# Where to sum the nine exponentials of batch 5: nine small TensorE products, or two VectorE reductions inside the gates of batch 4

## The chip, the cores and the metric

The kernel runs on one core of one Trainium2 chip. The metric is the time of one execution on the device in microseconds (us). Three runs of the kernel before took 235.49, 235.75 and 235.82 us; their median, 235.75 us, is the time that the change is held against.

A core has four computing engines that run side by side, each through its own instructions in their order. TensorE (PE) multiplies matrices; its weight loads are counted apart (PEld). VectorE (DVE) and ScalarE (ACT) work along rows of data, and both can read the accumulators (PSUM). GpSimd (POOL) does such work too. SyncE (SP) starts transfers (DMA). PSUM is used here as eight banks of 128 x 512 float32.

## The reference, cut to what matters

```python
def _attn_ref(q, k, v, phi):              # 8 batches, 8 heads, 576 positions, 64 wide; 32 memory slots
    a = phi - np.max(phi, axis=2, keepdims=True)
    a = np.exp(a)
    a = a / (np.sum(a, axis=2, keepdims=True) + 1e-09)      # sum over the 576 positions
    k_m = np.einsum('bhsm,bhsd->bhmd', a, k)
    v_m = np.einsum('bhsm,bhsd->bhmd', a, v)
    scores = np.matmul(q, k_m.transpose(0, 1, 3, 2)) / np.sqrt(64)
    ...                                   # softmax over the 32 slots
    return np.matmul(attn, v_m)

def _moe_ref(x, w_gate, w_val, w_out):    # 4608 tokens, 512 -> 1536 -> 512
    g = x @ w_gate
    silu = g * (1.0 / (1.0 + np.exp(-g)))
    return (silu * (x @ w_val)) @ w_out
```

The change concerns one sum: `np.sum(a, axis=2)`, for batch 5 alone. The kernel first adds up exp(phi)k and exp(phi)v, and divides by that sum afterwards.

## The kernel before, where the change touches it

The kernel goes through the batches one after the other. While the gates and values of batch b are computed, the memory sums of batch b+1 are slipped in between. In SBUF a head's 576 positions lie as 64 rows of 9 positions, two heads above each other in 128 rows, so that the exponentials of a batch are one tile `ephi` of 128 rows x 9 x (4 x 32). The sum over 576 positions is then a sum over the nine, followed by a sum over 64 rows, which a product with a matrix of ones does.

Banks of PSUM are taken from a queue and put back at its end, **in the order of the program text**. A product that takes a bank waits on the chip until its last user has read it.

```python
    free = [f"B{n}" for n in range(8)]
    def bank(shape, dtype, name):
        tag = free.pop(0)
        ...
    def done(*tiles):
        for t in tiles:
            free.append(held.pop(id(t))[0])
```

Where GpSimd adds the nine up, it leaves a pair: the sum rounded to bf16, and what the rounding lost. Where it doesn't (batches 2, 3 and 5), nine products do the whole sum.

```python
    def phi_sum(b):                                          # on GpSimd
        e = ephis[b].rearrange("p j i m -> p j (i m)")
        wait_for(atts[b - 1, 1][0:1, 0, 0:1])
        t = att.tile([128, 4, 128], FP32, tag="es", bufs=1, name="t_es")
        ...                                                  # 8 terms, then 4, 2, 1, then the ninth
        hl = att.tile([128, 2, 128], BF16, tag="ehl", bufs=1, name="t_ehl")
        nc.gpsimd.tensor_copy(out=hl[:, 0], in_=t[:, 0])
        nc.gpsimd.tensor_tensor(out=hl[:, 1], in0=t[:, 0], in1=hl[:, 0], op=ALU.subtract)
        esums[b] = hl

    def kv_denominators(b, p):                               # line 258
        ...
        if b in esums:
            hl = esums.pop(b)
            terms = [hl[:, t] for t in range(2)]             # two products
        else:
            terms = [ephis[b][:, j].rearrange("p i m -> p (i m)") for j in range(JK)]   # nine
        for n, x in enumerate(terms):
            nc.tensor.matmul(p, lhsT=x, rhs=ones2, start=(n == 0), stop=(n == len(terms) - 1))

    def kv_items(b, beside=None):
        def run_sums():
            o = 2 * D
            p = [bank([128, CH], FP32, f"p_kv{g}") for g in range(NG)]
            behind = b in esums
            if not behind:
                kv_denominators(b, p[0][:, o:o + NG])
            kv_sum(b, p, (0, 1))                             # line 230: 72 products
            if behind:
                beside()
                kv_denominators(b, p[0][:, o:o + NG])
            kv_reciprocal(b, p[0][:, o:o + NG])              # line 262, VectorE
            kv_norm(b, p)                                    # line 266: four VectorE copies, then done(p[g])
            if beside and not behind:
                beside()
        return [run_sums, lambda: kv_T(b)]
```

`beside()` is a round of products of the feed-forward weights with the memory values (line 465, four banks, emptied in the order ScalarE, ScalarE, VectorE, ScalarE: lines 485 and 489), and two units of output products (line 719). So `behind` settles more than a count: with it the banks `p_u` are emptied before the banks `p_kv`, without it after.

A slot of the gates: two products for the gate and a Silu on ScalarE (line 525), and for the slot before it two products for the value and a multiplication on VectorE (line 531). Each takes a bank and gives it back.

```python
    def gv_slot(b, s):
        n = len(pend)
        gv_gate(b, s)          # bank, 2 products, Silu, done(gate); the value's part is put in pend
        flush_mul(n)           # bank, 2 products, VectorE multiplication, done(val)
```

In the gates of batch 4 the output products of four batches' leftover rows (`quad`) run as well. Their first sum, `p_oa`, is taken from its bank by VectorE on line 788 (`leftover("c11")`), and GpSimd makes the twelve terms they need in `quad_sums(0)`, 128 x 256 each, as soon as `t_A` of batch 4 is there. The program of a batch is woven from streams by `spread`: every stream's items are set at even distances between two marks of the 24 slots.

```python
        g = gv_slots(b)
        ...
        streams = [(g, 0, 24), (quad[:12], 0, 3), (quad[12:], 12, 18.5)]
        streams += [(outs, 4, 7 if quad else 24)]
        ...
        if not last:
            if b > 2:
                load_qT(b + 1)
            if b > 2 and b != 4:
                phi_sum(b + 1)
            streams += [
                (kv_items(b + 1, lambda: (u_item(b, 2, "aava")(), run(take(2)))), KV, KV + 4),
                ...
            ]
        spread(*streams)
```

Of the kernel before, what the change touches and what calls it, by code (L numbers as in the profile page):

```python
# [9 lines left out]
FP32 = mybir.dt.float32  # L10
BF16 = mybir.dt.bfloat16
# [3 lines left out]
def kernel(  # L15
# [19 lines left out]
    nc = tc.nc  # L35
    AF = mybir.ActivationFunctionType
    ALU = mybir.AluOpType
# [18 lines left out]
    att = ctx.enter_context(tc.tile_pool(name="att", bufs=2))  # L56
# [57 lines left out]
    def load_qT(b):  # L114

        qTs[b] = att.tile([128, NS, 128], BF16, tag="qT", name="t_qT")
        nc.sync.dma_start_transpose(out=qTs[b], in_=qs[b])
# [50 lines left out]
    ephis, rSs, bkvs, kTs, es, atts = {}, {}, {}, {}, {}, {}  # L168

    def phi_exp(b):  # L170
        t = att.tile([128, JK, NP, M], BF16, tag="ephi", name="t_ephi")
        nc.scalar.activation(
            out=t.rearrange("p j i m -> p i j m"),
            in_=phis.pop(b).rearrange("p i (j m) -> p i j m", m=M),
            func=AF.Exp,
        )
        ephis[b] = t
# [25 lines left out]
    esums = {}  # L203

    def phi_sum(b):
# [6 lines that stand above are left out]
        add = lambda o, x, y: nc.gpsimd.tensor_tensor(out=o, in0=x, in1=y, op=ALU.add)  # L212
        add(t, e[:, 0:4], e[:, 4:8])
        add(t[:, 0:2], t[:, 0:2], t[:, 2:4])
        add(t[:, 0], t[:, 0], t[:, 1])
        add(t[:, 0], t[:, 0], e[:, 8])
        hl = att.tile([128, 2, 128], BF16, tag="ehl", bufs=1, name="t_ehl")
        nc.gpsimd.tensor_copy(out=hl[:, 0], in_=t[:, 0])
        nc.gpsimd.tensor_tensor(out=hl[:, 1], in0=t[:, 0], in1=hl[:, 0], op=ALU.subtract)
        esums[b] = hl  # L220

    def kv_sum(b, p, parts):


        w0, w1 = parts[0], parts[-1] + 1
        n = (w1 - w0) * D
        for j in range(JK):
            for i in range(NP):
                for g in range(NG):
                    nc.tensor.matmul(  # L230
                        p[g][32 * i:32 * i + 32, 0:n],
                        lhsT=phi_of(b, g, j, i),
                        rhs=kvs[b][64 * g:64 * g + 64, w0:w1, i, j * D:(j + 1) * D],
                        start=(j == 0),
                        stop=(j == JK - 1),
                        tile_position=(64 * g, 32 * i),
                    )
# [54 lines left out]
# [9 lines that stand above are left out]
            kv_sum(b, p, (0, 1))  # L301
# [3 lines that stand above are left out]
            kv_reciprocal(b, p[0][:, o:o + NG])  # L305
            kv_norm(b, p)
# [4 lines that stand above are left out]
# [241 lines left out]
    def subtract(eng, out, x, y):  # L552
        eng.tensor_tensor(out=out, in0=x, in1=y, op=ALU.subtract)  # L553

    def weight_sums(c, part=(0, 1, 2, 3)):

        if 0 not in part:
            t = Ts[c]
            for n in part:
                x, y = Ts[c, n]  # L560
                subtract(nc.vector, t[:, n], x, y)
            return
        home = dict(tag=f"mphi{c}", bufs=1) if c < 2 else dict(tag="T2", bufs=1)
        t = att.tile([128, 4, 2, DM // 2], BF16, name="t_T", **home)
        w = WOc[c].rearrange("p (m e) f -> p e m f", e=2)
        h = DM // 2
        B11, B12, B21, B22 = (w[:, e, :, h * n:h * n + h] for e in range(2) for n in range(2))
        Ts[c] = t
        for n, xy in enumerate(((B12, B11), (B22, t[:, 0]), (B22, B12), (B21, t[:, 1]))):
            Ts[c, n] = xy  # L570
            if n in part:
                subtract(nc.vector, t[:, n], *xy)
# [62 lines left out]
    def wait_for(x):  # L635

        t = att.tile([1, 1], BF16, tag="mark", bufs=1, name="t_mark")
        nc.gpsimd.tensor_copy(out=t, in_=x)
# [182 lines left out]
    def q_items(b, evac):  # L821
        return [lambda n=n: q_T(b, n, evac[n]) for n in range(3)]
# [13 lines left out]
    def u_values(b):  # L836

        u_round(b, (((1,), 1, (0, 1)),), "aa")
    def run(items):
        for x in items:  # L840
            x()
# [10 lines left out]
    def exp_tables():  # L852
        nc.scalar.preload_act_table_set("natural_log_exp_and_others")
# [111 lines left out]
    def take(n):  # L965
        nonlocal backlog
        n = max(0, min(n, len(backlog)))
        part, backlog = backlog[:n], backlog[n:]
        return part
# [3 lines left out]
    def loads(b):  # L973

        if b < B:
            load_q(b)
            load_phi(b, nc.gpsimd)
            load_k(b)
            load_v(b)
# [7 lines left out]
    for b in range(2, B):  # L987
        last = b + 1 == B
        exp_tables()
        if b == 2:  # L990
            load_qT(3)
            phi_exp(2)
            (zero, ops0), (one, ops1) = products(0, ("c11",)), products(1, ("p1", "c11"))
            kv, q2 = kv_items(2), q_items(2, "aaa")
            run(zero[:6])
            sums = {n: f for n, f in zip(((1, 1), (0, 2), (1, 2)), late)}
            late.clear()
            sums[0, 2]()
            weight_sums(0)
            weight_sums(1)  # L1000
            run(zero[6:12] + one[:6] + kv[:1] + q2[:2])
            weight_sums(2, (0, 1))
            run(zero[12:16] + zero[18:22] + kv[1:] + q2[2:] + zero[16:18] + zero[22:24])
            weight_sums(2, (2, 3))
            ops0["c11"]()
            ops1["p1"]()
            wait_for(Ts[2][0:1, 3, 0, 0:1])
            for part in ((0, 1), (3,), (2,)):
                for c in (1, 2):
                    sums[1, c](part)  # L1010
            loads(4)
            backlog = one[6:12] + zero[36:] + one[12:36]
            ops = ops1
        else:
            run(take(6))
        for g in range(NG):
            scores(b, g)
        if b > 2:
            ops["p1"]()
            u_values(b)  # L1020
        else:
            run(zero[24:36] + take(6))
        run(take(6))
        z_inv_v(b, 0)
        ops["c11"]()
        run(take(6))
        if not last:
            phi_exp(b + 1)
        z_inv_v(b, 1)
        if b > 2:  # L1030
            norm(b, 0)
            norm(b, 1)
        run(take(6))
        run_late()
        if b == 4:
            wait_for(atts[4, 1][0:1, 0, 0:1])
            quad_sums(0)
        nc.scalar.preload_act_table_set("silu_and_others")
        run(take(6))
        if b == 2:  # L1040
            norm(2, 0)
        run(take(6))
        if b == 2:
            norm(2, 1)
            u_three(2)
            run(one[36:])
        g = gv_slots(b)
        quad = []
        if b == 4:
            quad = products(b, (), 0)[0]  # L1050
        if last:
            rest, rest_ops = products(b, (), 1)
            backlog += rest[:12]
        beside = 0 if last else 2 if quad else min(4, len(backlog))
        outs = [lambda: run(take(1)) for _ in range(len(backlog) - beside)]
        streams = [(g, 0, 24), (quad[:12], 0, 3), (quad[12:], 12, 18.5)]
        streams += [(outs, 4, 7 if quad else 24)]
        if b == 2:
            streams += [([lambda: u_values(2)], 2.5, 3)]
        if last:  # L1060
            streams += [([u_item(b, 2)], 5, 6)]
        if not last:
            if b > 2:
                load_qT(b + 1)
            if b > 2 and b != 4:
                phi_sum(b + 1)
            streams += [
                (kv_items(b + 1, lambda: (u_item(b, 2, "aava")(), run(take(2)))), KV, KV + 4),
                ([lambda: (u_three(b + 1), run(take(2)))], 19, 20),
            ]  # L1070
        spread(*streams)
        flush_mul()
        units, ops = products(b, ("p1", "c11"))
        backlog += units
# [34 lines left out]
```

The softmax here doesn't subtract the row's maximum and nothing guards it: scores larger than these inputs give would overflow.

## Time and profile before

| what | before |
|---|---|
| time, median of 3 (lowest, highest) | 235.75 us (235.49, 235.82) |
| span of the profiled run | 233.8 us |
| TensorE busy (weight loads) | 224.5 us, 96% (169.9 us, 73%) |
| VectorE, ScalarE, GpSimd busy | 183.2 us (78%), 173.5 us (74%), 140.6 us (60%) |
| clock granted to TensorE | full in all 40 slices |
| line 258 with exponentials, 128 x 2 | 27 products, 163 ns each |
| line 258 with the pair, 128 x 2 | 6 products, 165 ns each |
| GpSimd term for `quad`, 128 x 256 bf16 | 658 ns each |

The profile page gives the busy time of each engine, the chain of work that ended last, and the costliest groups of instructions by source line. The timeline lists instructions in order of time: start in us from the span's start, length, engine, line, operation, what is written and read, the shape, and in brackets the idle time before it with what ended it. Equal neighbours are merged into one line with a count. Ends of products overlap the starts of the next ones, so lengths of TensorE are not added up: **differences of starts** tell its pace.

### The profile page before, as it was taken

What the parts mean: (1) busy time and instruction counts of PE and PEld (TensorE: products, weight loads), DVE (VectorE), ACT (ScalarE), POOL (GpSimd) and SP (SyncE); (2) the same over time, 40 slices, a digit from 0 to 9 for tenths busy, and PEclk for the clock granted to TensorE, in tenths of its full rate; (3) what the DMA queues carried; (4) which work ended last, traced back from release to release, by engine and by line L of the source; (5) the groups of instructions that cost most, each with busy time, mean ns of one, the idle gap of its engine ahead of it and who ended that gap; (6) DMA issues with size and microseconds to landing.
All of it is one profiled execution on the core that took longest, in us unless ns stands there. A gap on an engine that the chain in (4) does not pass through costs nothing.

```text
span 233.8 us, 7201 instructions
## 1 busy us (share of the span) xinstructions
PE 224.5 (96%) x2825; PEld 169.9 (73%) x2825; DVE 183.2 (78%) x421; ACT 173.5 (74%) x369; POOL 140.6 (60%) x190
## 2 busy tenths in 40 slices
PE   7997899999999999999999999999999999999992
PEld 2554466778887776878788787877788778878881
DVE  4056799999966698989797767999799879977732
ACT  2759798988547889968896658968897789677220
POOL 8422536998199059665966688464745494039390
PEclk9999999999999999999999999999999999999999
DMA  6999999999995993999199946995024502201224
GB/s 213 210 210 206 200 206 207 231 236 266 205 241 134 261 251 47 231 227 151 35 259 212 190 128 121 254 217 94 15 78 110 106 0 94 90 35 57 62 76 136
DMA packets 36610, 36.84 MB, mean 158 GB/s; under 512 B 14560, under 2 KB 30944, under 8 KB 36576
## 3 DMA queue, kind: packets, MB, share of 16 engines
q0 software_dynamic: 16272, 22.42, 51.5%
q1 hardware_dynamic: 19536, 13.18, 23.6%
q10 hardware_dynamic: 768, 0.79, 1.1%
q8 instruction: 22, 0.36, 0.6%
q14 instruction: 12, 0.10, 0.1%
HBM read 42.47 MB, written 9.44 MB: 222 GB/s over the span
## 4 chain that ended last, share of the span: by engine, by line
PE 88%; DMA 7%; POOL 1%; ACT 1%; DVE 1%; issue 1%; POOLq 0%
PE p_v L508 21%; PE p_g L508 21%; PE p_os L719 20%; PE p_oc L719 10%; DMA t_kv<-in_v_dram 7%; PE p_u L465 5%; PE p_oa L719 5%; PE p_kv L230 2%; PE p_g L389 1%; POOL t_kv L99 1%; PE p_mT L318 1%; PE p_warm L866 1%; PE p_q L376 0%; POOL t_q L108 0%; DVE t_kT L332 0%
## 5 line engine op out<-in xcount | busy, mean ns | idle before, releaser
L531 DVE TENSOR_TENSOR t_h<-t_sg,p_v 128x288 bf16<-128x288 bf16 x192 | 81.9, 452 | 17.3 <-PE p_v L508 7.4
L508 PEld LDWEIGHTS <-t_U 128*128 128x128 bf16 x768 | 73.6, 98 | 23.2 <-issue 3.8
L525 ACT ACTIVATE t_sg<-p_g 128x288 bf16<-128x288 f32 x192 | 74.0, 424 | 17.8 <-PE p_g L508 11.5
L508 PE MATMUL p_g<-t_A,t_U 128*128 128x288 bf16 x384 | 77.1, 286 | 0.5 <-ACT t_U L487 0.5
L508 PE MATMUL p_v<-t_A,t_U 128*128 128x288 bf16 x384 | 77.2, 286 | 0.0
L719 PEld LDWEIGHTS <-t_S 128*128 128x128 bf16 x384 | 37.5, 98 | 4.5 <-issue 0.2
L596 POOL TENSOR_TENSOR t_S<-t_h 128x512 bf16<-128x512 bf16 x17 | 19.6, 1155 | 32.5 <-DVE t_h L531 30.4
L719 PEld LDWEIGHTS <-t_h 128*128 128x128 bf16 x288 | 27.1, 98 | 8.6 <-issue 5.0
L485 ACT CAST t_U<-p_u 128x512 bf16<-128x512 f32 x53 | 28.0, 607 | 6.6 <-PE p_u L465 6.6
L719 PE MATMUL p_os<-t_T,t_S 128*128 128x256 bf16 x192 | 23.7, 273 | 0.0
L553 POOL TENSOR_TENSOR t_S<-t_S,t_h 128x512 bf16<-128x512 bf16 x17 | 19.6, 1154 | 1.3
L553 POOL TENSOR_TENSOR t_S<-t_h,t_S 128x512 bf16<-128x512 bf16 x16 | 18.4, 1151 | 0.0
L553 POOL TENSOR_TENSOR t_S<-t_h 128x512 bf16<-128x512 bf16 x16 | 18.4, 1150 | 0.0
L465 PE MATMUL p_u<-W,t_kT 64*32 64x512 bf16 (+1 forms) x416 | 15.8, 364 | 0.6 <-DVE t_kT L332 0.6
L866 PE MATMUL p_warm<-bones 128*128 128x512 bf16 x44 | 13.8, 457 | 1.7 <-DVE bones L888 1.7
L719 PE MATMUL p_os<-t_T,t_h 128*128 128x256 bf16 x96 | 14.8, 273 | 0.0
L489 DVE CAST t_U<-p_u 128x512 bf16<-128x512 f32 x19 | 12.4, 684 | 1.9 <-PE p_u L465 1.9
L445 DVE TENSOR_TENSOR t_A<-t_E,t_lz 128x576 bf16<-128x576 bf16 x16 | 11.4, 739 | 0.7 <-ACT t_lz L421 0.7
L719 PE MATMUL p_oc<-t_T,t_S 128*128 128x256 bf16 x96 | 12.0, 273 | 0.0
L719 PE MATMUL p_oa<-WO,t_h 128*128 128x256 bf16 x96 | 11.8, 273 | 0.0
L719 PE MATMUL p_oc<-WO,t_S 128*128 128x256 bf16 x96 | 11.8, 273 | 0.0
L719 PE MATMUL p_os<-WO,t_h 128*128 128x256 bf16 x96 | 11.8, 273 | 0.0
(106 smaller groups left out, 308.8 us busy)
## 6 DMA issues: line engine op xcount, KB each, us to landing
out_dram<-t_o SPq DMA_DIRECT2D x15, 512.0 KB, 3.8
t_kv<-in_k_dram POOLq DMA_DIRECT2D x8, 576.0 KB, 10.2
t_q<-in_q_dram POOLq DMA_DIRECT2D x8, 576.0 KB, 8.6
t_kv<-in_v_dram POOLq DMA_DIRECT2D x8, 576.0 KB, 14.9
t_phi<-in_phi_dram POOLq DMA_DIRECT2D x6, 576.0 KB, 8.3
WO<-in_moe_w_out_dram POOLq DMA_DIRECT2D x3, 512.0 KB, 19.3
W<-in_moe_w_gate_dram POOLq DMA_DIRECT2D x2, 512.0 KB, 16.4
W<-in_moe_w_val_dram POOLq DMA_DIRECT2D x2, 512.0 KB, 16.2
```

What stands on the lines that cost most here:

```text
L230: nc.tensor.matmul(p[g][32 * i:32 * i + 32, 0:n], lhsT=phi_of(b, g, j, i), rhs=kvs[b][64 * g:64 * g + 64, w0:w1, i, j * D:(j + 1) * D], st ...
L445: nc.vector.tensor_tensor(out=a, in0=es.pop((b, g)), in1=lzs.pop((b, g)), op=ALU.mult)
L465: nc.tensor.matmul(p[g][32 * i:32 * i + 32, o:o + n], lhsT=kTs[b][64 * g:64 * g + 64, 2, 32 * i:32 * i + 32], rhs=w_part(w, c, i, g, halve ...
L485: nc.scalar.copy(out=t, in_=p)
L489: nc.vector.tensor_copy(out=t, in_=p)
L508: nc.tensor.matmul(p[:, 0:HALF], lhsT=Us[b, c, g][:, o // 2, which, 128 * (o % 2):128 * (o % 2 + 1)], rhs=atts[b, g][:, r], start=(g == 0) ...
L525: nc.scalar.activation(out=sg, in_=gate[:, 0:HALF], func=AF.Silu)
L531: nc.vector.tensor_tensor(out=dst, in0=sg, in1=val[:, 0:HALF], op=ALU.mult)
L553: eng.tensor_tensor(out=out, in0=x, in1=y, op=ALU.subtract)
L596: eng.tensor_tensor(out=t[:, 0], in0=A21, in1=A22, op=ALU.add)
L719: nc.tensor.matmul(mine[home][:, u], lhsT=lhs(c, m, u), rhs=rhs(c, m), start=fresh and u == 0, stop=(k == 5), skip_group_check=u == 1 or n ...
L866: nc.tensor.matmul(p[:, 0:128 * a], lhsT=bones, rhs=x.to_broadcast([128, a, 128]) if a > 1 else bones, start=True, stop=True,)
```

## The change

GpSimd is taken up by `quad_sums` in the gates of batch 4, so batch 5 was left without the pair. The change has VectorE make it there instead: two reductions over nine elements, each of 64 of the 128 columns, a copy that rounds to bf16, and a subtraction. They are a stream of three items over the first three slots of the gates of batch 4. Since `esums` then holds batch 5, `kv_items` takes its `behind` branch for it as it does for batches 4, 6 and 7.

```diff
+    def phi_sum_items(b):
+        e = ephis[b].rearrange("p j i m -> p (i m) j")
+        t = att.tile([128, 4, 128], FP32, tag="es", bufs=1, name="t_es")
+        hl = att.tile([128, 2, 128], BF16, tag="ehl", bufs=1, name="t_ehl")
+        esums[b] = hl
+        def half(n):
+            cols = slice(64 * n, 64 * n + 64)
+            nc.vector.tensor_reduce(
+                out=t[:, 0, cols], in_=e[:, cols], axis=mybir.AxisListType.X, op=ALU.add
+            )
+        def split():
+            nc.vector.tensor_copy(out=hl[:, 0], in_=t[:, 0])
+            subtract(nc.vector, hl[:, 1], t[:, 0], hl[:, 0])
+        return [lambda: half(0), lambda: half(1), split]
...
-            if b > 2 and b != 4:
+            if b == 4:
+                streams += [(phi_sum_items(b + 1), 0, 3)]
+            elif b > 2:
                 phi_sum(b + 1)
```

As built, VectorE's program in these slots becomes: reduction, multiplication 0, reduction, multiplication 1, copy, subtraction, the sum of line 788, multiplications 2 to 5. Before it was: multiplications 0 and 1, line 788, multiplications 2 to 5. TensorE loses nine products ahead of the 72 of line 230 and gets two behind the products of `beside`. GpSimd's program is the same, and so is the order of the transfers.

## The prediction

> **What bounds the kernel now.** I read the chain of work that ended last first. Nearly all of it is TensorE, from about 21 us on almost without a break, so a microsecond that TensorE saves or loses near 130 us should reach the end.
>
> ```profile
> ## 4 chain that ended last, share of the span: by engine, by line
> PE 88%; DMA 7%; POOL 1%; ACT 1%; DVE 1%; issue 1%; POOLq 0%
> ```
>
> Then the timeline of TensorE about the memory sums of batch 5, which now begin with the nine products:
>
> ```profile
> 129.72 0.38 PE L719 MATMUL p_os<-t_T,t_h 128*128 128x256 bf16 x2
> 129.94 0.37 PE L258 MATMUL p_kv<-ones,t_ephi 128*128 128x2 bf16 x9
> 130.23 0.80 PE L230 MATMUL p_kv<-t_kv,t_ephi 64*32 64x128 bf16 x72
> 131.41 0.61 PE L719 MATMUL p_os<-t_T,t_h 128*128 128x256 bf16 x4
> 131.88 0.42 PE L508 MATMUL p_g<-t_A,t_U 128*128 128x288 bf16 x2
> 132.33 0.42 PE L508 MATMUL p_v<-t_A,t_U 128*128 128x288 bf16 x2
> ```
>
> The nine hold TensorE for 130.23 - 129.94 = 0.29 us. A pair of 288-wide products takes 0.245 us from start to start (111.81 and 112.05 in the same timeline), but the last two lines are 0.45 apart: 0.205 us is a stall. The waits list puts it down to VectorE's copies of `p_kv`, and the timeline of VectorE shows them filling 131.29 to 132.28. The bank of that value product is the second `p_kv` bank.
>
> The same passage for batch 4, whose pair GpSimd made, is the picture that the change aims at:
>
> ```profile
> 103.46 0.41 PE L508 MATMUL p_v<-t_A,t_U 128*128 128x288 bf16 x2
> 103.80 0.80 PE L230 MATMUL p_kv<-t_kv,t_ephi 64*32 64x128 bf16 x72
> 105.43 0.19 PE L258 MATMUL p_kv<-ones,t_ehl 128*128 128x2 bf16 x2
> 105.48 0.41 PE L508 MATMUL p_g<-t_A,t_U 128*128 128x288 bf16 x2
> 105.72 0.41 PE L508 MATMUL p_v<-t_A,t_U 128*128 128x288 bf16 x2
> ```
>
> Here the two cost 0.05 us and gate and value are 0.24 apart: no stall. But 0.095 us passes idle before the 72 (they could start at 103.46 + 0.245 = 103.705), which the nine now cover.
>
> Last, what VectorE and GpSimd do where the new work goes. In the first lines VectorE waits for the value products; the sum of line 788 follows on multiplication 1; GpSimd works without a pause, one term each (128.47 - 126.59) / 3 = 0.627 us:
>
> ```profile
> 126.23 0.45 DVE L531 TENSOR_TENSOR t_h<-t_sg,p_v 128x288 bf16<-128x288 bf16 x1 [0.59 <-PE p_v L508]
> 127.15 0.45 DVE L531 TENSOR_TENSOR t_h<-t_sg,p_v 128x288 bf16<-128x288 bf16 x1 [0.47 <-PE p_v L508]
> 127.53 0.42 DVE L788 TENSOR_TENSOR t_o<-p_oa,t_p 128x256 f32<-128x256 f32 x1
> 126.59 1.91 POOL L553 TENSOR_TENSOR t_Q<-t_Q,t_x 128x256 bf16<-128x256 bf16 x3
> 128.47 1.92 POOL L553 TENSOR_TENSOR t_x<-t_x 128x256 bf16<-128x256 bf16 x3
> ```
>
> **What the Trainium skill says.** "SBUF — State Buffer", section Who interferes with whom: VectorE and GpSimd share a pair of ports as an exclusive lock; a VectorE instruction with two SBUF inputs contends with a GpSimd instruction that reads SBUF, a copy may, and tensor_reduce never does. The trace has such a meeting: GpSimd's copies of `t_x` beside VectorE's sums `t_S`, both inputs of which lie in SBUF. The sum before the copies takes 0.42 us, those beside them 0.62 and 0.64, each ending about 0.3 us behind a copy's end, and the copies slow down too: the two engines take turns.
>
> ```profile
> 55.48 0.42 DVE L596 TENSOR_TENSOR t_S<-t_h 128x512 bf16<-128x512 bf16 x1
> 55.93 0.62 DVE L553 TENSOR_TENSOR t_S<-t_S,t_h 128x512 bf16<-128x512 bf16 x1
> 56.48 0.64 DVE L553 TENSOR_TENSOR t_S<-t_h 128x512 bf16<-128x512 bf16 x1
> 55.82 1.57 POOL L585 COPY t_x<-t_h 128x256 bf16<-128x256 bf16 x3
> ```
>
> "VectorE: DVE Perf Modes", sections on the errata and the tier table: tensor_reduce runs at one element a cycle, and an instruction at that rate lasts (N + 151) / 0.96 ns. For N = 576 that gives an estimate of 757 ns. The trace has no plain tensor_reduce, but three other forms over 576 elements agree: 764 ns for the transposing reduction, 778 for the transposition, 739 for the product `t_A`. The next instruction starts before the recorded end, some 0.07 to 0.08 us earlier (the transposition at 122.35 lasts 0.78, its follower starts at 123.06).
>
> **The change, part by part.** *On TensorE.* From the first free moment to the second of the two gate and value products: now 132.33 - 129.94 = 2.39 us; in the pattern of batch 4, 105.72 - 103.705 = 2.015 us. The saving is 0.375 us: nine products less two, 0.24; the stall, 0.205; against that the 0.095 of idle time that comes into the open; the rest, 0.025, is rounding and small gaps. All of it is on the path.
>
> *On VectorE,* estimates from the durations above. The last sum of the output products starts at 124.96 and lets a follower start at 125.56. Reduction 125.56 to 126.24 (757 ns less 0.08); multiplication 0 at 126.24, against 126.23 before; reduction from 126.61; multiplication 1 at 127.29, against 127.15; copy at 127.66. Up to here the idle gaps of 0.59 and 0.47 us take the work nearly whole. Now the split. If the ports were free: copy of 128 elements to 127.95 at most ((128 + 151) / 0.96 = 0.29 us), subtraction to about 128.25, line 788 from 128.17 to 128.59. With the ports taken: GpSimd's terms run from 127.22 to 127.87 and from 127.84 to 128.50. The copy comes out at about 127.97 either way (held until 127.87, then short; or not held, 0.29 us). The subtraction, asked for at 128.0, finds GpSimd in its next term and waits for its end at 128.50 to 128.58; it ends near 128.7, and line 788 runs from 128.65 to 129.07.
>
> *What line 788 sets free.* I follow the queue of banks. When the first `quad` sum has its bank, the queue is 3, 4, 7, 2, 0, 6. Gate 0 takes 3, gate 1 takes 4, value 0 takes 7, `p_oa` takes 2, gate 2 takes 0, value 1 takes 6; the banks come back in the order 3, 4, 7, 0, 6, 2. So gate 3 and value 2 take 3 and 4, gate 4 and value 3 take 7 and 0, gate 5 takes 6, and **value 4 takes bank 2**, which line 788 frees. Value 4 starts at 128.76 now. From the end of a bank's reader to the product is about 0.055 us (the last `p_kv` copy ends at 132.28, the product starts at 132.33). So line 788 may end by 128.70. Free ports: 128.59, no stall. Taken ports: 129.07 + 0.055 = 129.12, a stall of 0.36 us, or 0.29 if the copy leaves GpSimd's term alone. The banks of multiplications 2 and 3 come free by about 129.5 and 129.9 and are asked for again near 129.8 and 130.4: in time.
>
> *The sum.* Free ports: -0.375 us. Taken ports: -0.375 + 0.29 to 0.36, that is -0.02 to -0.09. In both cases a change within two tenths of a percent.
>
> **The rivals.**
> 1. *The whole gain arrives* (-0.4 us): 235.4. For it: tensor_reduce stays off the shared ports, and 0.11 us is in hand when nothing contends. The lock may also be held for less than a GpSimd term's recorded 0.66 us, so that the subtraction slips in.
> 2. *The stall moves* from the `p_kv` bank to bank 2, and the gain is nearly used up: 235.65 to 235.75. For it: GpSimd is busy without a gap in just this window, and the meeting at 56 us shows the turn-taking. Against it: that was a copy, this is a GpSimd sum.
> 3. *The reductions are slower than one element a cycle,* since each reads nine elements 128 apart and writes 64 results. At 0.9 us each from start to start, multiplication 1 slips to 127.74, the copy meets the next term, the subtraction the one after it, and line 788 ends near 129.75: a stall of about 1.0, the time near 236.4. Against it: the other reading forms over 576 elements keep to the estimate.
> 4. *TensorE's gain is hidden anyway,* behind a transfer or GpSimd. Against it: the transposing transfer of batch 5's keys is issued at 135.26, behind stores that SyncE issues first, three us after its data were ready, and its first reader comes at 141.84; GpSimd has nearly 2 us idle after its terms (1.96 before 134.22).
>
> **Range and chances.** I give the first rival 35%, the second 45%, the third 15%, the fourth 5%. Weighted with -0.37, -0.06, +0.5 and 0 that is -0.08, so I predict 235.65 us. The three runs before are spread over 0.33 us, so the medians add some 0.15 us. The range is 235.2 to 236.1. Nothing here moves the time by 2%, which would be 4.7 us: faster 0.005, within 2% 0.985, slower 0.01.
>
> **What the changed profile would show.** Right: no stall between the first gate and value after the two products, their starts 0.24 to 0.26 us apart; about 1.78 us from TensorE's first free moment to that gate, against 1.94 before; reductions of 0.74 to 0.78 us; multiplication 0 still at 126.2. The second rival shows as a subtraction of more than 0.5 us and a gap before value 4 on TensorE, ended by line 788; the first as a subtraction of about 0.3 us and no such gap; the third as reductions of 0.9 us or more. The prediction is wrong if value 4 waits for over 0.8 us, if the multiplications of VectorE still lag when `p_u` is emptied, or if the saving near 132 us is gone again by the scores of batch 5 near 145 us.

## The result, and the profile after

The changed kernel takes **241.77 us** (median of six runs, 241.22 to 242.39), the kernel before 235.78 us beside it. The ratio is 1.0255, with a 95% interval of 1.0236 to 1.0273. The prediction was 235.65 us, in a range up to 236.1.

The chain of work that ended last, of the changed kernel: TensorE's share falls from 88% to 78%, and VectorE's rises from 1% to 6%.

```profile
PE 78%; DMA 8%; DVE 6%; POOL 2%; issue 2%; ACT 2%; DVEq 0%; POOLq 0%; ACTq 0%
```

The timeline of VectorE in the gates of batch 4 shows the new instructions (line numbers from 222 on are 19 higher than before):

```profile
125.49 1.15 DVE L231 TENSOR_REDUCE t_es<-t_ephi 128x64 f32<-128x576 bf16 x1
...
126.92 1.14 DVE L231 TENSOR_REDUCE t_es<-t_ephi 128x64 f32<-128x576 bf16 x1
127.97 0.45 DVE L550 TENSOR_TENSOR t_h<-t_sg,p_v 128x288 bf16<-128x288 bf16 x1
128.34 3.94 DVE L236 CAST t_ehl<-t_es 128x128 bf16<-128x128 f32 x1
132.31 0.29 DVE L572 TENSOR_TENSOR t_ehl<-t_es,t_ehl 128x128 bf16<-128x128 f32 x1
132.52 0.42 DVE L807 TENSOR_TENSOR t_o<-p_oa,t_p 128x256 f32<-128x256 f32 x1
```

The copy of 128 columns is recorded with 3.94 us. The timeline of GpSimd in the same passage:

```profile
128.41 1.91 POOL L572 TENSOR_TENSOR t_x<-t_x 128x256 bf16<-128x256 bf16 x3
130.28 1.91 POOL L572 TENSOR_TENSOR t_Q<-t_x,t_Q 128x256 bf16<-128x256 bf16 x3
```

Its last term ends at 130.28 + 1.91 = 132.19; the copy ends at 128.34 + 3.94 = 132.28, 0.09 us later. Line 807 is line 788 of before: it frees bank 2 five us later than it did. On TensorE's timeline value 4 stands behind it. First gate 5 and value 4 before, then the same passage after:

```profile
128.52 0.41 PE L508 MATMUL p_g<-t_A,t_U 128*128 128x288 bf16 x2
128.76 0.41 PE L508 MATMUL p_v<-t_A,t_U 128*128 128x288 bf16 x2
```

```profile
128.48 0.40 PE L527 MATMUL p_g<-t_A,t_U 128*128 128x288 bf16 x2
132.99 0.64 PE L527 MATMUL p_v<-t_A,t_U 128*128 128x288 bf16 x2 [4.11 <-DVE t_o L807]
...
133.85 0.68 PE L527 MATMUL p_g<-t_A,t_U 128*128 128x288 bf16 x2
134.33 0.68 PE L527 MATMUL p_v<-t_A,t_U 128*128 128x288 bf16 x2
```

In the changed kernel they are 4.51 us apart where 0.245 is usual: 4.27 us of waiting. Behind it a gate and its value are 0.48 apart and last 0.68, not 0.41. The table by stage says why: its columns are the busy time of each engine (with the number of instructions), and behind them the granted clock of TensorE, the DMA share and GB/s.

```profile
128.00:132.70 4.70, 0.88 (x8) 0.58 (x6) 4.67 (x5) 0.82 (x2) 4.19 (x7) 1.00 1.18 182
132.80:136.10 3.30, 3.11 (x70) 2.02 (x74) 1.77 (x5) 0.41 (x1) 0.00 (x0) 0.50 0.63 139
136.20:139.00 2.80, 2.63 (x60) 1.69 (x41) 2.01 (x7) 2.26 (x6) 0.00 (x0) 1.00 0.01 1
```

TensorE works at half clock from 132.81 to 136.22 us, for 3.41 us. I compared the starts of the gates and values in the two traces. From 26 us up to this passage the changed kernel leads by a constant 0.06 us. Value 4 then starts 4.23 us late, the lag reaches 5.76 us at the gate at 138.84, and it is 5.76 up to the last product. So the passage costs 5.76 + 0.06 = 5.82 us, and nothing after it gives or takes. Each trace here has such a constant lead or lag from 26 us up to the passage, at most 0.3 us, which arises ahead of 26 us; where a passage is weighed below, it is taken off.

### The profile page after: what moved, and what is told of

Same layout as the page of the kernel before. It is cut to its first block, busy times and chain, and to the rows that moved or that the text cites. A ratio compares the mean times of both kernels' runs of the same rounds, so it can differ in the third digit from the quotient of the medians.

```text
span 239.6 us, 7193 instructions
## 1 busy us (share of the span) xinstructions
PE 225.6 (94%) x2818; PEld 170.3 (71%) x2818; DVE 189.4 (79%) x425; ACT 173.8 (73%) x369; POOL 140.6 (59%) x190
## 4 chain that ended last, share of the span: by engine, by line
PE 78%; DMA 8%; DVE 6%; POOL 2%; issue 2%; ACT 2%; DVEq 0%; POOLq 0%; ACTq 0%
PE p_v L527 20%; PE p_g L527 19%; PE p_os L738 18%; PE p_oc L738 9%; DMA W<-in_moe_w_gate_dram 8%; PE p_u L484 5%; PE p_oa L738 4%; PE p_kv L249 2%; DVE t_ehl L236 2%; DVE t_h L550 1%; DVE t_o L768 1%; POOL t_kv L99 1%; POOL t_kv L103 1%; DVE t_z L447 1%; PE p_g L408 1%
## 5 line engine op out<-in xcount | busy, mean ns | idle before, releaser
L738 PE MATMUL p_os<-t_T,t_h 128*128 128x256 bf16 x96 | 15.3, 279 | 0.0
L885 PE MATMUL p_warm<-bones 128*128 128x512 bf16 x44 | 13.3, 444 | 1.7 <-DVE bones L907 1.7
```

The lines of the kernel that those rows point to most:

```text
L738: nc.tensor.matmul(mine[home][:, u], lhsT=lhs(c, m, u), rhs=rhs(c, m), start=fresh and u == 0, stop=(k == 5), skip_group_check=u == 1 or n ...
L885: nc.tensor.matmul(p[:, 0:128 * a], lhsT=bones, rhs=x.to_broadcast([128, a, 128]) if a > 1 else bones, start=True, stop=True,)
```

## The experiments

Theory A: VectorE's copy is kept from the SBUF ports that it shares with GpSimd until GpSimd's row of terms has ended. Theory B: the copy waited for something in its own chain. Theory C: the slow reductions cost the time. Each run is held against runs of the kernel before on the same chip, medians between 235.65 and 235.86 us; where there is only one run of a kernel, the text says so.

### The copy alone

```diff
 # in the kernel before; the sum of batch 4 was finished at 104 us
+            if b == 4:
+                spare = att.tile([128, 2, 128], BF16, tag="ehl", bufs=1, name="t_ehl")
+                streams += [([lambda: nc.vector.tensor_copy(
+                    out=spare[:, 0], in_=sums_kept[4][:, 0])], 2, 3)]
```

> The kernel before, with one VectorE copy more: 128 columns of the pair's float32 sum of batch 4, long finished, rounded into a tile that nobody reads, at the place of the changed kernel's copy (behind multiplication 1 of the gates of batch 4). No reductions, no subtraction, nine products kept. Theory A (the copy is kept from the SBUF ports that VectorE and GpSimd share until GpSimd has run through all its back-to-back terms for the leftover rows): the copy is recorded with more than 4 us, value 4 waits about 4 us for the bank that line 788 frees, TensorE's clock falls to half for 3.4 us afterwards, and the time is 241 to 242. Theory B (the copy of the changed kernel waited for something of its own chain, reductions or tiles): the copy takes 0.25 to 0.3 us and the time stays within 0.2 us of before. Theory C (the slow reductions cause the loss): as B.

Measured: 241.11 us, ratio 1.0234 (1.0209 to 1.026). The copy on VectorE's timeline:

```profile
127.77 4.81 DVE L1070 CAST t_ehl<-t_es 128x128 bf16<-128x128 f32 x1
```

GpSimd's last terms are these:

```profile
130.59 1.91 POOL L554 TENSOR_TENSOR t_Q<-t_x,t_Q 128x256 bf16<-128x256 bf16 x3
```

The copy ends at 132.58, GpSimd's last term at 132.50. Its data were ready and nobody read its result. One copy of 128 columns makes nine tenths of the loss; B and C fall.

### The reductions alone

```diff
 # the changed kernel without the pair: half(0) and half(1) stay, nine products do the sum
-        return [lambda: half(0), lambda: half(1), split]
+        return [lambda: half(0), lambda: half(1)]
-                streams += [(phi_sum_items(b + 1), 0, 3)]
+                streams += [(phi_sum_items(b + 1), 0, 2)]
```

> The kernel before, with the two reductions alone in the gates of batch 4, at their places; their result is not read, the nine products do the sum. Theory A (copy and ports): 1.14 us each as in the changed kernel, line 788 ends near 128.75, a stall of 0.1 us at most for value 4, time 235.7 to 236.0. Theory C (the reductions cause a good part of the loss): 237 or more.

Measured: 235.77 us, ratio 1.0004 (0.9995 to 1.0012). The reductions take 1.15 us each beside GpSimd's terms, and 1.13 with GpSimd idle (the run with the terms after the pair): they aren't kept out. Value 4 comes 0.33 us behind gate 5, so it waits 0.09. Late as they are, they nearly fit into VectorE's idle time: the passage costs 0.12 us in this trace, too little for the time to show.

### The rounding without a copy

```diff
-            nc.vector.tensor_copy(out=hl[:, 0], in_=t[:, 0])
+            with nc.allow_low_precision(reason="one element each"):
+                nc.vector.tensor_reduce(
+                    out=hl[:, 0], in_=t[:, 0].rearrange("p (c a) -> p c a", a=1),
+                    axis=mybir.AxisListType.X, op=ALU.add,
+                )
```

> The changed kernel, but the rounding to bf16 is done by a reduction over one element per column in place of the copy; everything else is the same. Theory A, narrow form (only an instruction that needs both shared ports is kept out, and one with two SBUF inputs takes turns with GpSimd): rounding 0.3 us, subtraction at most 0.7 us, line 788 ends near 129.7, value 4 waits 0.9 us, clock stays full, time 236.2 to 236.8. Theory A, wide form (whatever uses a shared port waits for the last term): the subtraction takes over 3 us instead and the time is 241 to 242. Theory C: 240 or more with both short.

Measured: 241.5 us, ratio 1.0248 (1.0227 to 1.0268): the wide form.

```profile
128.56 0.29 DVE L237 TENSOR_REDUCE t_ehl<-t_es 128x128 bf16<-128x128 f32 x1
128.89 3.68 DVE L576 TENSOR_TENSOR t_ehl<-t_es,t_ehl 128x128 bf16<-128x128 f32 x1
```

The reduction in the copy's place is through in 0.29 us. Now the subtraction, with its two SBUF inputs, waits instead, to 132.57; GpSimd's last term ends at 132.42.

### The terms after the pair

```diff
-            wait_for(atts[4, 1][0:1, 0, 0:1])
-            quad_sums(0)
...
+                def split_then_terms():
+                    split()
+                    wait_for(pair[0:1, 1, 0:1])      # GpSimd waits for the pair
+                    quad_sums(0)
```

> The changed kernel, but GpSimd starts its twelve terms only when the pair is there, some 4 us later. Theory A: copy 0.2 to 0.3 us, subtraction 0.3 us, line 788 ends near 129.2, value 4 waits 0.5 us, time 235.9 to 236.5; the terms end near 136.7, still ahead of the products that read them. Theory B: the copy stays near 4 us and the time near 241.5. Theory C: 238 or more, with short copy and subtraction.

Measured: 236.46 us, ratio 1.0026 (1.0016 to 1.0037). With GpSimd idle the copy is short, and the wait for bank 2 shrinks from 4.27 to 129.52 - 128.72 - 0.245 = 0.56 us:

```profile
128.59 0.22 DVE L236 CAST t_ehl<-t_es 128x128 bf16<-128x128 f32 x1
```

```profile
128.72 0.41 PE L527 MATMUL p_g<-t_A,t_U 128*128 128x288 bf16 x2
129.52 0.40 PE L527 MATMUL p_v<-t_A,t_U 128*128 128x288 bf16 x2 [0.39 <-DVE t_o L807]
```

The clock stays full. What remains of the loss, 0.65 us, is this wait and what the gates behind the pair lose (see the pair on GpSimd, below).

### A row of six, a break, a row of six

```diff
-            quad_sums(0)
+            quad_sums(0, (0, 1))                     # six terms
...
+                    split()
+                    wait_for(pair[0:1, 1, 0:1])
+                    quad_sums(0, (2, 3))             # the other six
```

> The changed kernel, but GpSimd stops after six of its twelve terms, near 128.45, until VectorE has made the pair, and makes the other six then. If VectorE's copy is kept out until a row of GpSimd instructions has its end (and not by anything else of the window): the copy, asked for at about 128.35, ends within 0.3 us of the sixth term's end, the subtraction takes 0.3 us, value 4 waits 0.5 to 0.7 us, the clock stays full, and the time is 236.2 to 236.8. If the copy waits for the last term or for another thing of the window: the copy still takes over 3 us, and as GpSimd itself waits for the pair the time is 242 or more.

Measured: 236.44 us, ratio 1.0032 (1.0019 to 1.0044). The sixth term ends at 128.38; the copy, asked for at 128.28, takes 0.23 us and the subtraction 0.29. It had to wait for very little, as it was asked for just at the row's end; but it didn't wait for anything else in the window. With a row that ends at 128.38 the copy is through at 128.51, with one that ends at 132.19 it lasts to 132.28: the row's end decides. That a break lets in a copy which is already waiting, no run shows.

### Copies in place of the terms

```diff
 # quad_sums: each of the four kinds of term becomes a copy, made twice; the sums are left out
-                    nc.gpsimd.tensor_tensor(out=t[:, 0], in0=A21, in1=A22, op=ALU.add)
+                    nc.gpsimd.tensor_copy(out=t[:, 0], in_=A21)
```

> The changed kernel, but GpSimd's twelve sums and differences for the leftover rows are copies of one input, each made twice, 24 in all of about 0.37 us, to some 133.5 us. It leaves the sums out, so the leftover rows of batches 0 to 3 come out otherwise. Theory A1 (the form of GpSimd's instruction decides: back-to-back two-input instructions hold the shared ports, and copies give them up after each): VectorE's copy lasts 0.3 to 0.7 us, the subtraction 0.5 to 0.8, they and the copies beside them take turns, value 4 waits about 1 us, time 236.3 to 237. Theory A2 (any unbroken row of GpSimd instructions that read SBUF keeps VectorE out until its end): copy and subtraction together last until the row's end near 133.5 and the time is 241 to 243.

Measured: 242.96 us, ratio 1.0301 (1.0285 to 1.0316). VectorE's copy lasts 4.59 us, to 133.16; GpSimd's last copy ends at 133.08. Theory A2: a row of copies keeps VectorE's copy out as a row of sums does. The subtraction came after the row and met nothing, so a second run puts it in the row, by rounding with the reduction of above:

> As the run in which GpSimd makes 24 copies instead of twelve sums and differences (which leaves those sums out), but VectorE rounds by a reduction over one element per column, so that the subtraction alone meets the row of copies. Theory A3 (a two-input VectorE instruction takes turns with copies, as the sums t_S did at 56 us in the kernel before; only one that needs both ports waits for the end of a row of copies): the subtraction lasts 0.3 to 0.7 us, value 4 waits 1 us, time 236.3 to 237. Theory A2 (any row without a break, whatever its form): subtraction over 3.5 us, time 241 to 243.

Measured: 242.66 us, ratio 1.0294 (1.0277 to 1.0311); the subtraction lasts 4.31 us. A3, turns between copies and a two-input instruction, falls as well.

### Why was 56 us different?

The prediction had a precedent, the sums `t_S` that took turns with GpSimd's copies near 56 us. Three single runs tried its features one by one: the bf16 form of the sum, the interleaving form of the copies, and VectorE coming first.

```diff
 # in the kernel before, at the place of the copy alone (first and second run)
+                    nc.vector.tensor_tensor(out=spare[:, 0:512], in0=x, in1=y, op=ALU.add)   # x, y: t_A, bf16
 # second run: 24 GpSimd copies t_Q<-t_h of the form of t_x<-t_h; the twelve terms are left out
 # third run: six such sums on VectorE right behind t_A of batch 4
```

> The kernel before, with one VectorE sum more behind multiplication 1 of the gates of batch 4: both inputs and the result bf16, 128 x 512, the form of the sums t_S that took turns with GpSimd at 56 us in the kernel before. If the subtraction of the changed kernel was kept out for its float32 input or its small size: the sum lasts 0.42 to 0.9 us, time 235.6 to 236.6. If any two-input form is kept out: over 4 us, time 240.5 to 241.5.

> As the run with one two-input VectorE sum alone, but GpSimd's row consists of 24 copies of the very form that took turns at 56 us (128 x 256 out of t_h, two halves interleaved), in place of the twelve terms, which are left out (the leftover rows of batches 0 to 3 come out otherwise). If that form of copy is what let VectorE in: the sum lasts 0.5 to 0.9 us. If not: it lasts to the end of the row, over 4 us, and the time is 240.5 to 243.

> The kernel before, with six such VectorE sums in a row right behind t_A of batch 4, so that VectorE's row is running when GpSimd's row of twelve terms begins, as at 56 us. If the order decides (the row that is running is joined in turns): sums of 0.5 to 1.1 us each in alternation with terms that last longer than 0.66 us. If GpSimd's row holds the ports whatever came first: the sum that is running or waiting when the row begins lasts about 7 us, to the row's end, and the time is over 242.

Measured: 241.58, 244.27 and 247.16 us, beside 235.74 for the kernel before. The sum lasts 5.01, 6.16 and, as the second of the six in the third run, 7.78 us, each time to the end of GpSimd's row:

```profile
124.81 7.78 DVE L1037 TENSOR_TENSOR t_spare<-t_A 128x512 bf16<-128x512 bf16 x1
```

In this third run the first sum (124.35, 0.42 us) ran before the row and even held up GpSimd's little mark copy, which took 0.37 us in place of 0.18. GpSimd's first term began at 124.78, 0.03 us ahead of the second sum, which stood until 132.59, the last term having ended at 132.31; the other four took 0.42 us each. So neither the bf16 form, nor the interleaving copies, nor a row of VectorE's that runs first brings turns. Interleaving copies against a row of VectorE's, and a row of only three copies, were not run. What made the three copies at 56 us give way is **not settled**.

### Work for TensorE in the wait

```diff
+    def fill(n):
+        tag = free.pop(-1)                # second run: free.pop(2), the bank of gate 3
+        p = ps.tile([128, DM], FP32, tag=tag, name="p_fill")
+        for _ in range(n):
+            nc.tensor.matmul(p, lhsT=bones, rhs=x, start=True, stop=True)    # x: bones four times, 128 x 512
...
+                streams += [([lambda: fill(17)], 5.2, 5.2)]
```

> The changed kernel, with 17 products of 128 x 512 more ahead of gate 5, into a bank that nobody reads: some 3.7 us of work for TensorE in the time in which it waits for line 788 anyway. If the loss of about 5.8 us is a wait of 4.3 and, after it, TensorE at half clock for 3.4 us: the clock stays full in the slice behind the wait, value 4 still starts near 133, and the time is 239.8 to 240.6. If the clock has no part in the loss: 241.2 to 242.

Measured: 246.78 us, ratio 1.0464 (1.0435 to 1.0493), a miss. The bank was that of value 3, whose multiplication stood behind VectorE's copy too: the 17 products began only at 133.56, and, at half clock to 138.98, they took 6.49 us. It says nothing of the question. The second run takes a bank that ScalarE empties:

> As the run with the filled wait, whose 17 products themselves waited for VectorE: their bank was that of value 3. Here they go into the bank of gate 3, which ScalarE has long emptied, and so should run from about 128.5 to 132.2 while value 4 waits for line 788 as before. If TensorE's half clock after the wait is a part of the loss: full clock in the slices from 130 to 137, value 4 near 133, time 239.9 to 240.6. If not: 241.2 to 242.

Measured: 240.13 us, ratio 1.0183 (1.0165 to 1.0201). TensorE's timeline, and below it the granted clock from the page:

```profile
128.79 3.83 PE L901 MATMUL p_fill<-bones 128*128 128x512 bf16 x17
132.46 0.41 PE L527 MATMUL p_g<-t_A,t_U 128*128 128x288 bf16 x2
133.33 0.41 PE L527 MATMUL p_v<-t_A,t_U 128*128 128x288 bf16 x2 [0.47 <-DVE t_o L807]
```

```profile
PEclk9999999999999999999999999999999999999999
```

Value 4 starts as late as ever, 8.27 us behind gate 0 (125.06 here, 124.72 in the changed kernel), but the clock stays full, and 241.77 - 240.13 = **1.64 us** of the loss are gone. They were the price of the half clock. In the profiled executions it is less: the passage costs 4.40 us here and 5.82 in the changed kernel, 1.42 between them. The price seems to differ from one execution to the next: the six of the changed kernel run from 241.22 us at a mean clock of 0.991 to 242.39 at 0.981.

### The pair on GpSimd

```diff
 # in the kernel before
         if b == 4:
-            wait_for(atts[4, 1][0:1, 0, 0:1])
+            phi_sum(5)
             quad_sums(0)
 # second run, besides: the pair's two products ahead of the 72
-            behind = b in esums
+            behind = b in esums and b != 5
```

> The kernel before, but GpSimd makes batch 5's pair too, ahead of its terms for the leftover rows; no VectorE work is added. The nine products become two behind the products of beside. It shows what the part on TensorE is worth alone. The prediction's step: no stall after the two products, 0.375 us won, 235.4. What the traces since have shown: the gates behind meet the banks of the feed-forward products and of the leftover rows' sum instead, and wait twice for 0.25 us, so that 0.1 us is left, 235.7.

> As the run with the pair made by GpSimd first, but the two products of the pair stand ahead of the 72, where the nine stood, so that the banks come back in the order of the kernel before. Expected: 0.24 us less for the products, 0.1 us of idle time ahead of the 72 that the nine covered, the one stall of 0.2 us as before: 235.65, at most 0.1% from before.

Measured: 235.61 us, ratio 0.9989 (0.9982 to 0.9995), and 235.51 us, ratio 0.9985 (0.9978 to 0.9992), the two lowest medians of all. The pair is ready at 128.4 us, and the terms, 3.6 us later than before, still come in time. In the first of the two, TensorE behind the pair:

```profile
131.46 0.19 PE L258 MATMUL p_kv<-ones,t_ehl 128*128 128x2 bf16 x2
131.53 0.41 PE L508 MATMUL p_g<-t_A,t_U 128*128 128x288 bf16 x2
132.02 0.40 PE L508 MATMUL p_v<-t_A,t_U 128*128 128x288 bf16 x2
...
132.51 0.41 PE L508 MATMUL p_v<-t_A,t_U 128*128 128x288 bf16 x2
133.00 0.41 PE L508 MATMUL p_g<-t_A,t_U 128*128 128x288 bf16 x2
```

Gate and value are 0.49 apart, and value and gate 0.49 once more: two waits of 0.245 us in place of the one of 0.205. By the queue of banks the first is for the second bank of `p_u`, which ScalarE has emptied at 131.97; the second is for the bank of a sum of output products, whose copy on ScalarE ends at 132.95. Each product starts 0.05 us behind.

At the last product TensorE is 0.08 us ahead of before in this trace, but at gate 0 it already led by 0.19 (124.59 for 124.78), so the passage **loses** 0.11 us. That is the 0.375 of the prediction less the two waits, 0.49; the expectation above calls it a gain of 0.1, with the wrong sign. In the second run TensorE lags by 0.06 at gate 0 and leads by 0.12 at the end: with the banks in their old order the passage gains 0.18. The medians lie 0.25 and 0.35 us below before; what is more than the passage gives doesn't arise in it, and no run shows where it does.

### The nine elements side by side

```diff
 # the reductions alone, but over other elements; nobody reads the sums
-        e = ephis[b].rearrange("p j i m -> p (i m) j")
+        e = ephis[b].rearrange("p j i m -> p (j i m)").rearrange("p (c n) -> p c n", n=JK)
```

> As the run with the reductions alone, but each of the 64 sums of a half is taken over nine elements that lie side by side, not 128 apart (other sums, which nobody reads). If the distance of the elements makes the reduction slow: 0.74 to 0.8 us each instead of 1.15. If it is the form of the instruction (nine elements to a result): 1.1 to 1.2 us. Time in both cases 235.5 to 236.1.

Measured in one run: 235.75 us, beside 235.77.

```profile
125.31 0.74 DVE L229 TENSOR_REDUCE t_es<-t_ephi 128x64 f32<-128x576 bf16 x1
```

The distance of the elements makes the difference, 0.74 against 1.15 us.

## Why the prediction was wrong

**What held.** TensorE's chain carries a loss of this passage to the end undiminished (5.76 us from 138.84 us to the last product). Line 788 frees the bank of value 4, and it is what value 4 waits for. The 0.055 us from a bank's last reader to its next product came back (132.94 to 132.99). Nothing was hidden by transfers or GpSimd.

**The step that failed** is "The copy comes out at about 127.97 either way (held until 127.87, then short; or not held, 0.29 us)", with its sequel for the subtraction, "waits for its end at 128.50 to 128.58". Both take it that GpSimd gives the ports back after each term. The Trainium skill's page "SBUF — State Buffer", section Who interferes with whom, speaks of a lock for the whole instruction, and the meeting at 56 us looked like that. The runs showed VectorE kept out for the whole **row**: a copy or a two-input instruction of VectorE waited for the last of GpSimd's back-to-back instructions in six combinations (copy, subtraction and bf16 sum, each against sums and against copies), 3.7 to 7.8 us long. That it is the shared ports is inferred from what was kept out and what wasn't; whether GpSimd keeps them between its instructions, or takes them again each time ahead of VectorE, no run tells. The prediction had the right instruction, ports, bank and reader, and had the wait as one term of 0.63 us where it was all that was left of twelve. Its own sign of being wrong, a wait of value 4 over 0.8 us, came with 4.27. I weighed one precedent as if it were the rule; the unbroken row in the profile, and a third rival that already let the copy slip by a term, should have made me ask what happens if VectorE never gets its turn, and widen the range by those 4 us.

**The clock wasn't in the sum at all.** After 4.27 us without work TensorE ran at half clock for 3.41 us; by the filled wait it cost 1.64 us in the medians. The Trainium skill's page "TensorE: Matmul & The Clock Gate", Part 1, states that the clock halves after an idle window of about 3.4 us: the trace agrees in kind and length. No rival reckoned with a wait so long.

**The stall did not go away.** "No stall between the first gate and value after the two products" was read off batch 4's gates, but with the leftover rows' sums in their banks the queue here is empty after the feed-forward products: the gates have to wait for those very banks. Worth 0.375 us in the prediction, TensorE's part is a loss of 0.11 us in the passage. With the pair's products left ahead of the 72 it is a gain of 0.18. (The times of these two runs are 0.1% and 0.15% lower, which the passage explains in part at most.)

**The reductions** take 1.15 us, not 0.757: the third rival named the cause, the distance of 128 elements, rightly, and gave it 15%. (The formula behind 0.757 is given, on the page that the prediction names, for a sum of two float32 tensors; carried over to a reduction it comes close with the nine side by side, 0.74, and not with the nine apart.) The rival overrated what they cost: alone they cost 0.12 us in the passage, though in the changed kernel they put multiplication 1 off to 127.97.

The loss adds up in the traces: 4.27 us of waiting, 1.42 of half clock and 0.11 for TensorE's part are 5.80, and the passage costs 5.82.

## What to carry to other kernels

Before putting a VectorE copy or a two-input instruction beside GpSimd, look for how long GpSimd's row runs **without a break**, not how long one of its instructions is, and ask who waits for VectorE's next instruction; the reductions here weren't kept out. If a row can't be avoided, order it after the VectorE work or give the work to GpSimd ahead of the row. A wait on TensorE can cost more than its length: after those of 4.0 us and more it ran at half clock for a time, while a gap of 1.4 us (at 18.47 us in the run of the reductions alone) left the clock full; no run has one between. An order of banks read off a neighbouring stage holds only if as many banks are free there.

## What the runs showed of the hardware

- GpSimd instructions that follow each other directly (terms of 0.66 us, copies of 0.39) kept VectorE's copy, subtraction and bf16 sum out until the row's end, which they outlasted by 0.08 to 0.3 us. Against a sum already running, a GpSimd copy of one element waited once (0.37 for 0.18 us). The turns at 56 us remain unexplained.
- Reductions weren't held up: 1.15 us beside the row, 1.13 without it.
- A reduction over nine bf16 elements 128 apart takes 1.15 us for 576 elements, side by side 0.74. The Trainium skill's "SBUF — State Buffer", section Door 1: The DMA port swizzle, speaks of 16-byte lines that want to be hit at least twice in a row, which would fit; the two distances measured don't prove it.
- After 4.27 us of idling TensorE ran at half clock for 3.41 us; in the run with the rounding by reduction, after a wait of 4.0 us, for 6.83 us; in the run with six sums, after 8.4 us, for 10.24 us. These are one, two and three times 3.41. In the run of the copy alone, with a wait of 4.0 us, the half clock came only 1.1 us after TensorE had resumed.
